# A fused attention and expert kernel: eleven and five relu buffers in the bias stage, conversions that begin later in two blocks, and gating rows one step later

## The chip, the core and the metric

The kernel runs on one core of a Trainium2 chip. The metric is the device time in microseconds (us) of one execution. The core has five engines that each work through their own instructions in program order: TensorE (PE in the profile; its weight loads are PEld), VectorE (DVE), ScalarE (ACT), GpSimd (POOL), and SyncE, whose queue (SPq) issues nearly all transfers of this kernel. Engines wait for each other through semaphores, so an instruction that waits holds up everything behind it on the same engine.

## The reference, cut to what matters

Three parts follow each other. Attention with a computed position bias:

```python
x = (psi_rel / psi_i)[..., None]            # (576, 576, 1)
bias = np.maximum(x @ w1 + b1, 0.0) @ w2    # hidden 32, 8 heads
scores = scale * q @ k.T + bias.transpose(2, 0, 1)[None]
attn = softmax(scores); attn_out = attn @ v # batch 4, heads 8, seq 576, dim 64
```

Then a mixture of 8 experts that picks the best expert of each token and weighs the result by two gates, and then a dense layer pair on 2304 tokens:

```python
e_idx = argmax(x @ w_gate); gate_w = softmax(x @ w_gate)[e_idx]
out[t] = gate_w[t] * sigmoid(x @ w_output_gate)[e] * (relu(x @ w1[e]) @ w2[e])
h = x @ w_in; out = (h * cos(h)) @ w_out     # 512 -> 2048 -> 512, weights in float64
```

## The kernel before

**Bias stage** (`bias_table`). For 36 groups of rows, in the order ROWS, it makes four relu tiles of up to 128 x 576 (L379 on ACT into buffers hhA, L381 on DVE into buffers hhD), multiplies them with w2 on PE (L391), copies the result to a buffer `ev` on ACT (L363, five buffers in turn) and sends it to the table Bd in DRAM (L364). There are 8 buffers hhD and 4 hhA. The pools p0 (W, cc, bp), p0h (hhD, hhA) and p0e (ev) lie one behind the other in SBUF. When the stage ends they are given up, and attention's pools p1s (s, e, et) and p1e (eT0, eT1) take the same addresses. A tile that takes over an address waits for the last user of that address, which for `ev` is the transfer L364. By tile sizes (per partition): W, cc, bp 3,744 bytes; one hh 2,304; one ev 2,368; p1s 25,312; one eT 12,800. So eT0 lies at 25,312 to 38,112 of this region and eT1 at 38,112 to 50,912, and the five ev at 31,392 to 43,232. The last row group (position 35) uses the first ev buffer.

**Attention** (`attention`). 16 pairs n (two heads hp of a batch b) of 5 units u each. One pass over a unit: scores on PE (L524), bias add and row minimum on DVE (L534), then for the unit before it transposes on PE (L560) and copies of them into eT0 or eT1 on ACT and DVE (L571, L573), exponentials on ACT (L545), the product with V on PE (L607), and the transposed rests (L593, L599). PSUM holds the scores of one unit, so the scores of the next unit wait for this unit's L534. Pair 0's bias comes from Bd by L440 and L443; its split into high and low parts runs on POOL.

**Later** is a list of work with due times. `later.step()` moves the clock by one and runs what is due: nine steps per pair (two in units 0 to 3, one in unit 4), then one for each step of the expert block. Work due at 0 and at 1 after it is queued runs in the same step. `Later` also holds chains, which `drip` emits a few instructions at a time and `drain` emits at once.

**Gating** (`Gating.queue`) is queued for batch b when the last product with V of its last pair is made, in unit 2 of the pair behind it (pairs 10, 12 and 14 for b = 0, 1, 2; for b = 3 just ahead of the expert block). Its parts: `sums` (DVE, L186 to L189: reciprocals rs of the row sums), `rows` (PE L196 and L197 turn rs, ACT L199 and L200 copy it to the buffer lp, SP sends it to Fd), `factors` (loads F from Fd, L207), `scale` (L213), `logits0` (PE L224, ACT L225 into lp), `logits1` (L232, L233) and the chain `choose`, which ends with L295 on PE and the copy L297 on ACT into lp. There is one buffer lp. `logits0` of batch b first drains the chain of b - 1.

**Conversions** (`Doubles.half`). The weights of the last part come as float64 in 64 pieces. A piece takes two halves: L712 and L714 on DVE; L717 and L719 on DVE, L721 on POOL, a store (L722) and the load of a later piece (L701) on SP. Attention takes 24 pieces: `convert` emits 4 halves in a pair (CV_AT). The expert block takes the other 40.

**Expert block** (`moe_dense`). 64 steps s of 12 matmuls of layer 1 (L854) and 12 of layer 2 (L873, two steps behind). ACT (L858) and DVE (L859) turn a step's output into high and low parts, and L803 splits weights on DVE. A counter `dense.cost` adds planned DVE time; from step CONVERT_AT on, halves of 0.73 are emitted as long as the counter stays within STEP:

```python
while cv and cv.u < cv.end and (dense.cost + 0.73 <= STEP or least > 0):
```

The last part (`moe2`, PE work by L1379 and L1419) is not touched.

Of the kernel before, what the change touches and what calls it, by code (L numbers as in the profile page):

```python
# [9 lines left out]
F32 = mybir.dt.float32  # L10
# [9 lines left out]
B, H, S, D = 4, 8, 576, 64  # L20
# [100 lines left out]


SPREAD_AT, PAUSE = 40, (10, 14)
GATE_AT = (4, 4, 11, 12, 10, 11, 17, 18, 20), (4, 4, 5, 6, 5, 6, 7, 8, 12)


class Gating:
# [42 lines left out]
    def queue(self, later, b):  # L170

        at = GATE_AT[b == B - 1]
        p = [(0, self.sums), (1, self.rows)]
        p += [(at[i], lambda b, i=i: self.factors(b, i)) for i in range(NP_)]
        p += [(at[4 + i], lambda b, i=i: self.scale(b, i)) for i in range(NP_)]
        p += [(at[8] + i, lambda b, i=i: (later.drain(b - 1), self.logits0(b, i))) for i in range(2)]
        p += [(at[8] + 2, self.logits1),
              (at[8] + 3, lambda b: later.chains.append((b, self.choose(b))))]
        start = max(0, self.clear - later.now)
        self.clear = later.now + start + 12  # L180
        later.add([(dt, lambda fn=fn: fn(b)) for dt, fn in p], start)
# [124 lines left out]
def reach(G):  # L306

    return 16 * G + 15, S - 16 * G
# [23 lines left out]
def bias_table(tc, h, Bd, first, after):  # L332


    nc = tc.nc
    NQ = S // 4
    with tc.tile_pool(name="p0", bufs=1) as c, \
         tc.tile_pool(name="p0h", bufs=10) as hp_, \
         tc.tile_pool(name="p0e", bufs=5) as ep, \
         tc.tile_pool(name="p0ps", bufs=3, space=PSUM) as pp:  # L340
        W = c.tile([128, S], F32, name="W")
        cc = c.tile([128, 34 + NQ + S // 16], F32, name="cc")
        near, far = slice(0, 336), slice(336, S)
        nc.sync.dma_start(out=W[:, near], in_=h["t_rel"][:, near])
        nc.scalar.dma_start(out=cc, in_=h["cc"])
        nc.sync.dma_start(out=W[:, far], in_=h["t_rel"][:, far])
        first()
        w1c, b1c, w2b, psi, rp8 = cc[:, 0:1], cc[:, 1:2], cc[:, 2:34], cc[:, 34:34 + NQ], cc[:, 34 + NQ:]
        bp = c.tile([128, NQ], F32, name="bp")
        nc.vector.tensor_scalar(out=bp, in0=psi, scalar1=b1c, scalar2=None, op0=ALU.mult)  # L350
        slope = lambda t: nc.vector.tensor_scalar(out=W[:, t], in0=W[:, t], scalar1=w1c, scalar2=None, op0=ALU.mult)
        slope(near)
        pss = {}

        def evac(G):
            back, ahead = reach(G)
            ev = ep.tile([128, S + 15], F32, name="ev")
            ps, zero = pss.pop(G)
            parts = [(ev[:, 0:back + ahead], ps[:, zero - back:zero + ahead])]
            if G in MIRROR:  # L360
                parts = [(ev[:, 0:back], ps[:, 1:back + 1][:, ::-1]), (ev[:, back:back + ahead], ps[:, 0:ahead])]
            for dst, src in parts:
                nc.scalar.activation(out=dst, in_=src, func=AF.Copy, scale=rp8[:, G:G + 1])  # L363
            nc.sync.dma_start(out=Bd[:, 16 * G:16 * G + 16, S - 1 - back:S - 1 + ahead].rearrange("h i j -> i h j"),  # L364
                              in_=ev[:, 0:back + ahead])
            after(G)

        for at, G in enumerate(ROWS):
            ps = pp.tile([128, 1024], F32, name="ps")
            back, ahead = reach(G)  # L370
            n = max(back + 1, ahead)
            hs = []
            for ct in range(4):
                m = 4 * G + ct
                e = BIAS_ON[m]
                hh = hp_.tile([128, S], F32, name="hh" + e, bufs=dict(D=8, A=4)[e])
                hs.append(hh)
                if e == "A":
                    nc.scalar.activation(out=hh[:, 0:n], in_=W[:, 0:n], func=AF.Relu, bias=bp[:, m:m + 1], scale=1.0)  # L379
                else:  # L380
                    nc.vector.tensor_scalar(out=hh[:, 0:n], in0=W[:, 0:n], scalar1=bp[:, m:m + 1], scalar2=0.0,  # L381
                                            op0=ALU.add, op1=ALU.max)
            zero = 512 if max(back, ahead) <= 512 else back
            cuts = sorted({zero - back, zero, 512, zero + ahead})
            if G in MIRROR:
                zero, cuts = 0, [0, n]
            pss[G] = ps, zero
            for c0, c1 in zip(cuts, cuts[1:]):
                for ct in range(4):
                    x = hs[ct][:, c0 - zero:c1 - zero] if c0 >= zero else hs[ct][:, zero - c1 + 1:zero - c0 + 1][:, ::-1]  # L390
                    nc.tensor.matmul(ps[32 * ct:32 * ct + 32, c0:c1], w2b, x, start=True, stop=True)  # L391
            if at == 2:
                slope(far)
            if at >= 2:
                evac(ROWS[at - 2])
        evac(ROWS[-2])
        evac(ROWS[-1])


def attention(tc, h, ident, dram, xT, bpool, ps_t, gate, later, dense, cv):  # L400
# [3 lines left out]
    with ExitStack() as ctx:  # L404
# [90 lines left out]
        def first():  # L495
            load(0)
            load_v(0)

        bias_table(tc, h, Bd, first, after)
        sp, ep = pool("p1s", 3, **rw), pool("p1e", 1, **rw)  # L500
        ps_s, ps_a = pool("ps_s", 2, space=PSUM, **rw), pool("ps_a", 1, space=PSUM)
        gate.pa = [ps_a.tile([128, 512], F32, name=f"pa{g}") for g in range(2)]
        ET = []
        for g in range(2):
            e = ep.tile([128, 5, 2, 320], F32, name=f"eT{g}")
# [109 lines left out]
                        later.add([(SPREAD_AT, lambda: (later.drain(b), gate.spread(b)))])  # L615

        def convert(n, u):
            for _ in range(CV_AT[u] if cv and n < 12 else 0):
                cv.half()

        seq = [(n, u) for n in range(len(pairs)) for u in range(NU)]
# [3 lines left out]
        while t <= len(seq) or av:  # L625
            n, u = seq[t] if t < len(seq) else (None, None)
# [43 lines left out]
            if n is not None:  # L670
                if u < 4:
                    convert(n, u)
                    later.step()
                later.drip(2)
# [6 lines left out]
CV_AT = (0, 1, 0, 1, 2)  # L681
# [281 lines left out]
            later.step()  # L963


STEP, CONVERT_AT = 3.1, 6
X_AT, X2_AT, ADD_AT, GROUP_AT, HALF_AT, NEXT_AT = 21, 34, 48, 57, 60, 61
W1_AT = (3, 17, 39, 49)
W2_AT = (7, 21, 44, 53)
# [548 lines left out]
```

## Time and profile before

| what | value |
|---|---|
| median of 3 runs | 984.64 us (983.89 to 988.12) |
| profiled execution: own time | 988.05 us |
| profiled execution: span from first to last instruction | 986.3 us |
| mean granted TensorE clock, share of 2.4 GHz | 0.976 |
| PE busy in the span | 939.6 us (95%) |
| DVE busy | 663.5 us (67%) |
| ACT busy | 547.1 us (55%) |

The span has four stages: bias 0 to 46 us, attention 46 to 326 us, the expert block 326 to 579 us, the last part 579 to 986 us. In a line of the timeline the numbers ahead are start and duration; what stands in brackets at the end is how long the engine had been idle before it and what ended that.

### The profile page before, as it was taken

To read this page: it belongs to the slowest core of one execution; us is meant where nothing else is said; L and a number is where in the kernel's file an instruction comes from. 1 tells how busy PE (TensorE), PEld (TensorE's weight loads), DVE (VectorE), ACT (ScalarE), POOL (GpSimd) and SP (SyncE) were. 2 spreads that over 40 slices of the span, in tenths; PEclk is the share of its full clock that TensorE was granted. 3 is DMA by queue.
4 is the path that set the end of the run, shared out by engine and by line. 5 is a ranking of instruction groups with operands and counts; after the bars stand their busy time and mean duration, and the time that the engine had idled before them with its cause. 6 is when DMAs were issued, how large, how long until landed. Compare 5 with 4: busy or idle time off the path is not lost.

```text
span 986.3 us, 19359 instructions
## 1 busy us (share of the span) xinstructions
PE 939.6 (95%) x7185; PEld 794.1 (81%) x7186; DVE 663.5 (67%) x1498; ACT 547.1 (55%) x1171; POOL 303.7 (31%) x414
## 2 busy tenths in 40 slices
PE   7979999989989896999999999999999999999997
PEld 4656666666666695999989998999999989999996
DVE  8958888988676466887658989654454454544542
ACT  8947777777667522335234377545455454554443
POOL 0034554545344211221321114324224233232222
PEclk9969999999999997999999999999999999999999
DMA  7965536643525393553765734010010010100001
GB/s 217 284 204 190 156 126 211 197 135 115 163 87 173 104 298 132 185 179 118 219 226 191 265 119 137 22 64 1 1 64 1 18 47 1 64 1 1 33 1 37
DMA packets 62101, 118.07 MB, mean 120 GB/s; under 512 B 6649, under 2 KB 21261, under 8 KB 61997
## 3 DMA queue, kind: packets, MB, share of 16 engines
q1 hardware_dynamic: 61708, 116.58, 36.8%
q8 instruction: 59, 0.97, 0.4%
q14 instruction: 46, 0.37, 0.1%
q10 hardware_dynamic: 288, 0.16, 0.1%
HBM read 83.11 MB, written 33.60 MB: 118 GB/s over the span
## 4 chain that ended last, share of the span: by engine, by line
PE 67%; DVE 5%; issue 2%; DMA 2%; ACT 1%; POOL 1%; SPq 0%; DVEq 0%; ACTq 0%; POOLq 0%
PE ph L1379 20%; PE py L1419 20%; PE pl L854 8%; PE po L873 8%; PE ps_s L524 2%; PE pa L607 2%; DMA F<-Fd 1%; PE Tp L560 1%; DVE s L534 1%; PE Tp L1151 1%; PE Tp L1160 1%; DMA raw<-in_w_in 1%; DVE xT L213 0%; DVE f32a L714 0%; DVE w0l L803 0%
## 5 line engine op out<-in xcount | busy, mean ns | idle before, releaser
L1405 POOL TENSOR_TENSOR gl<-tg,gh 128x384 fp32r<-128x384 f32 x96 | 97.8, 1019 | 280.6 <-ACT gh L1404 166.9
L1314 ACT ACTIVATE tk<-ph,magic 128x384 f32<-128x384 f32 x96 | 55.6, 579 | 159.0 <-PE ph L1379 158.5
L1319 DVE TENSOR_SCALAR tk<-tk 128x384 f32<-128x384 f32 x96 | 36.8, 383 | 154.2 <-ACT tk L1314 154.2
L1379 PE MATMUL ph<-xh,w0l 128*128 128x384 f32 x384 | 129.5, 337 | 0.0
L1379 PE MATMUL ph<-xh,w0h 128*128 128x384 f32 x384 | 129.2, 336 | 0.0
L1379 PE MATMUL ph<-xl,w0h 128*128 128x384 f32 x384 | 129.2, 336 | 0.0
L545 ACT ACTIVATE e<-s,mn 128x576 f32<-128x576 f32 x144 | 110.2, 768 | 9.1 <-DVE mn L534 8.6
L721 POOL TENSOR_TENSOR f32a<-f32a,raw 128x256 f32<-128x256 f32 x64 | 48.2, 754 | 212.7 <-DVE raw L719 171.3
L1419 PE MATMUL py<-w1h,gl 128*128 128x512 f32 x288 | 113.2, 393 | 0.0
L1419 PE MATMUL py<-w1h,gh 128*128 128x512 f32 x288 | 113.0, 392 | 0.0
L1419 PE MATMUL py<-w1l,gh 128*128 128x512 f32 x288 | 112.9, 392 | 0.0
L534 DVE CUSTOM_DVE_ANT_0 s<-ps_s,Bp 128x576 f32<-128x576 f32 x112 | 80.9, 755 | 35.2 <-PE ps_s L524 28.9
L607 PE MATMUL pa<-eT,V 128*64 128x256 f32 (+1 forms) x640 | 96.4, 423 | 0.0
L524 PE MATMUL ps_s<-HL 64*128 64x288 f32 x768 | 78.7, 324 | 6.6 <-DVE mn L534 4.3
L524 PEld LDWEIGHTS ps_s<-HL 64*128 64x128 f32 x768 | 59.6, 195 | 29.2 <-DVE mn L534 12.7
L854 PE MATMUL pl<-xh,w0h 128*128 128x288 f32 x256 | 79.9, 312 | 1.4 <-ACT xh L825 1.0
L858 ACT ACTIVATE hh<-pl 128x288 fp32r<-128x288 f32 x64 | 26.3, 411 | 99.0 <-PE pl L854 98.9
L854 PE MATMUL pl<-xl,w0h 128*128 128x288 f32 x256 | 76.3, 298 | 0.4 <-DVE xl L827 0.4
L854 PE MATMUL pl<-xh,w0l 128*128 128x288 f32 x256 | 76.1, 297 | 0.0
L873 PE MATMUL po<-hh,w1l 128*128 128x288 f32 x256 | 75.7, 296 | 0.0
L873 PE MATMUL po<-hh,w1h 128*128 128x288 f32 x256 | 75.7, 296 | 0.0
L873 PE MATMUL po<-hl,w1h 128*128 128x288 f32 x256 | 75.6, 295 | 0.0
(223 smaller groups left out, 2253.7 us busy)
## 6 DMA issues: line engine op xcount, KB each, us to landing
Bp<-in_w SPq DMA_DIRECT2D x38, 512.0 KB, 5.2
Bd<-ev SPq DMA_DIRECT2D x36, 295.5 KB, 3.6
Rqk<-in_qk SPq DMA_DIRECT2D x16, 576.0 KB, 6.4
raw<-in_w_in SPq DMA_DIRECT2D x32, 256.0 KB, 4.1
raw<-in_w_out SPq DMA_DIRECT2D x32, 256.0 KB, 3.2
Bp<-Bd SPq DMA_DIRECT2D x28, 288.0 KB, 6.8
X<-xT SPq DMA_DIRECT2D x7, 1152.0 KB, 5.3
V<-in_v SPq DMA_DIRECT2D x16, 320.0 KB, 4.5
```

What stands on the lines that cost most here:

```text
L524: nc.tensor.matmul(p[:, hf, :HF], w, y, start=(x == 0), stop=(x == 2))
L534: nc.vector.tensor_tensor_reduce(out=h2(s), in0=ps[:, :, :HF], in1=h2(bias(hp, i)), scale=-0.125, scalar=3e38, op0=ALU.add, op1=ALU.min, a ...
L545: nc.scalar.activation(out=e[:, par, :], in_=s, func=AF.Exp, bias=mn, scale=-1.0, accum_out=acc)
L607: nc.tensor.matmul(pa[64 * par:64 * par + 64, :W], d["V"][:, k, par, :], ET[g][:, k, par, :W], start=(k == 0), stop=(k == 4))
L721: self.tc.nc.gpsimd.tensor_tensor(out=af[:], in0=af[:], in1=low, op=ALU.add)
L854: nc.tensor.matmul(ps[:, :HF], w[:, c, :], x[:, c, :], start=(n == 0), stop=(n == 3 * NP_ - 1))
L873: nc.tensor.matmul(self.acc[d][:, :HF], w[:, ds_], x, start=(f == 0 and n == 0), stop=(f == self.FC - 1 and n == 2))
L1314: nc.scalar.activation(out=k, in_=hh, func=AF.Identity, scale=INV2PI, bias=magic)
L1319: nc.vector.tensor_scalar(out=k, in0=k, scalar1=-MAGIC, scalar2=None, op0=ALU.add)
L1379: nc.tensor.matmul(ps[:, :GT], w[:, c, :], x[:, c, :], start=(n == 0), stop=(n == 3 * NP_ - 1))
L1405: nc.gpsimd.tensor_tensor(out=lo, in0=g, in1=hi.bitcast(F32), op=ALU.subtract)
L1419: nc.tensor.matmul(acc[t], x[:, ts_], w, start=(f == 0 and n == 0), stop=(f == FC - 1 and n == 2))
```

## The change

Five edits: the relu buffers hhD go from 8 to 11 and hhA from 4 to 5, which moves the five `ev` buffers up by 9,216 bytes; the conversions of attention run in pairs 1 to 12 and not in 0 to 11; `rows` is due 2 steps after `sums` is queued and not 1; `logits0`, `logits1` and `choose` of batches 0 to 2 come one step later (20 to 21); conversions in the expert block begin at step 10 and not 6, with a planned fill of 3.2 and not 3.1 per step.

```diff
-GATE_AT = (4, 4, 11, 12, 10, 11, 17, 18, 20), (4, 4, 5, 6, 5, 6, 7, 8, 12)
+GATE_AT = (4, 4, 11, 12, 10, 11, 17, 18, 21), (4, 4, 5, 6, 5, 6, 7, 8, 12)
...
-        p = [(0, self.sums), (1, self.rows)]
+        p = [(0, self.sums), (2, self.rows)]
...
-                hh = hp_.tile([128, S], F32, name="hh" + e, bufs=dict(D=8, A=4)[e])
+                hh = hp_.tile([128, S], F32, name="hh" + e, bufs=dict(D=11, A=5)[e])
...
-            for _ in range(CV_AT[u] if cv and n < 12 else 0):
+            for _ in range(CV_AT[u] if cv and 0 < n < 13 else 0):
                 cv.half()
...
-STEP, CONVERT_AT = 3.1, 6
+STEP, CONVERT_AT = 3.2, 10
```

## Rows read from the trace of the kernel before

**Rows 1.** Windows: stretch: length, busy us (instructions) by engine, PE clock, DMA share, GB/s.

```profile
4.70:46.00 41.30, 41.02 (x556) 25.66 (x560) 41.30 (x117) 38.76 (x69) 0.00 (x0) 1.00 0.85 261
50.00:72.00 22.00, 15.24 (x132) 11.49 (x134) 12.15 (x29) 10.03 (x24) 7.25 (x13) 0.61 0.62 204
365.00:400.00 35.00, 26.66 (x186) 24.15 (x186) 24.04 (x70) 10.58 (x21) 6.44 (x7) 0.85 0.41 136
400.00:450.00 50.00, 49.48 (x376) 49.03 (x375) 43.40 (x120) 19.28 (x37) 14.99 (x15) 1.00 0.63 195
578.80:986.30 407.50, 400.91 (x2016) 363.53 (x2015) 216.97 (x403) 211.10 (x429) 119.76 (x116) 1.00 0.10 31
```

**Rows 2.** Waits of the whole span: engine, line, waited for: total us, times, longest.

```profile
PE pa L196 <- DVE rs L187: 6.0, 3, 2.1
```

**Rows 3.** Timeline of pair 0 of attention, 49 to 66 us.

```profile
49.86 0.76 SPq L364 DMA_DIRECT2D Bd<-ev  x1
...
50.67 2.57 SPq L440 DMA_DIRECT2D Bp<-Bd  x3
...
53.94 2.48 PE L524 MATMUL ps_s<-HL 64*128 64x288 f32 x12
...
56.73 0.60 ACT L571 ACTIVATE eT<-Tp 128x512 f32<-128x512 f32 x1 [4.21 <-DMA Bd<-ev]
...
62.48 0.29 DVE L712 TENSOR_SCALAR f32a<-raw 128x256 int32<-128x256 int32 x1 [4.94 <-DMA raw<-in_w_in]
62.80 0.42 DVE L714 SCALAR_TENSOR_TENSOR f32a<-raw,f32a 128x256 int32<-128x256 int32 x1
63.15 0.75 DVE L534 CUSTOM_DVE_ANT_0 s<-ps_s,Bp 128x576 f32<-128x576 f32 x1
```

**Rows 4.** Source L440 up to 62 us: time of the bias loads from issue to landing.

```profile
DMA to landing us min/median/max: 4.0/6.6/6.8
```

**Rows 5.** Timeline of DVE in pair 9: L534 of units 2 and 3.

```profile
201.11 0.76 DVE L534 CUSTOM_DVE_ANT_0 s<-ps_s,Bp 128x576 f32<-128x576 f32 x1 [0.66 <-PE ps_s L524]
...
204.19 0.76 DVE L534 CUSTOM_DVE_ANT_0 s<-ps_s,Bp 128x576 f32<-128x576 f32 x1 [0.23 <-ACT xT L610]
```

**Rows 6.** Timeline of pair 10, units 2 and 3.

```profile
216.40 0.76 DVE L534 CUSTOM_DVE_ANT_0 s<-ps_s,Bp 128x576 f32<-128x576 f32 x1 [0.67 <-PE ps_s L524]
...
220.47 0.71 PE L196 MATMUL pa<-ident,rs 128*8 128x128 f32 x5 [2.13 <-DVE rs L187]
...
222.98 0.76 DVE L534 CUSTOM_DVE_ANT_0 s<-ps_s,Bp 128x576 f32<-128x576 f32 x1 [2.43 <-PE ps_s L524]
```

**Rows 7.** Timeline of pair 14, units 3 and 4.

```profile
295.11 0.76 DVE L534 CUSTOM_DVE_ANT_0 s<-ps_s,Bp 128x576 f32<-128x576 f32 x1 [2.63 <-PE ps_s L524]
...
296.69 0.27 ACT L297 ACTIVATE lp<-pa 5x128 f32<-5x128 f32 x1 [2.37 <-DMA Fd<-lp]
...
301.57 0.76 DVE L534 CUSTOM_DVE_ANT_0 s<-ps_s,Bq 128x576 f32<-128x576 f32 x1 [4.41 <-PE ps_s L524]
```

**Rows 8.** Timeline of PE in the first steps of the expert block.

```profile
331.28 1.23 PE L196 MATMUL Tp<-ident,rs 128*8 128x128 f32 x5 [2.01 <-DVE rs L187]
...
333.08 0.61 PE L854 MATMUL pl<-xh,w0h 128*128 128x288 f32 x1
```

**Rows 9.** Timeline of the expert block, steps 6 to 11: DVE and PE.

```profile
357.47 0.76 DVE L213 TENSOR_TENSOR xT<-xT,F 128x576 f32<-128x576 f32 x1 [3.46 <-DMA F<-Fd]
...
363.30 0.88 DVE L714 SCALAR_TENSOR_TENSOR f32a<-raw,f32a 128x256 int32<-128x256 int32 x1
...
370.98 0.29 DVE L712 TENSOR_SCALAR f32a<-raw 128x256 int32<-128x256 int32 x1 [2.70 <-DMA raw<-in_w_in]
...
375.07 0.39 PE L269 MATMUL Tp<-oh,ones 128*128 128x40 f32 x2 [3.86 <-DVE oh L256]
...
378.16 0.19 DVE L272 TENSOR_REDUCE cnt<-Tp 128x8 f32<-128x40 f32 x1
...
379.94 0.37 PE L295 MATMUL Tp<-ident,cs 128*5 128x128 f32 x1 [4.48 <-DVE cs L289]
```

## The prediction

> **What bounds the kernel now.** I read the windows by stage first [rows 1]. In the last part PE is busy 400.91 of 407.5 us, with nothing of the change in it, and at 400 to 450 us, deep in the expert block, 49.48 of 50. In both PE sets the end, so an edit can gain there only what PE idles: almost nothing. In the bias stage DVE is busy all 41.30 us and PE follows it. What is left is three places where PE stands still: pair 0 of attention (50 to 72 us: 15.24 of 22, clock 0.61), the gating rows of each batch, and steps 9 to 12 of the expert block (365 to 400 us: 26.66 of 35, clock 0.85). The list of waits names the second kind: PE waits for rs, the row sums' reciprocals, 6.0 us in three places [rows 2]. Then I read the timelines of these places, in order of time.
>
> **Pair 0.** The exact chain [rows 3]: the last ev transfer is issued at 49.86; ACT's first copy into eT0 waits until 56.73 for it, since eT0 (25,312 to 38,112) lies on ev buffers, the first of which (31,392 to 33,760) is the one sent last. DVE's copy waits too. Behind that copy DVE has the first conversion half, which waits until 62.48 for raw, and behind this the L534 of unit 2, at 63.15, though PE had its scores ready at 56.4 (53.94 + 2.48).
>
> More relu buffers put ev at 40,608 to 52,448. eT0 then overlaps only relu buffers, whose readers are matmuls that are over; eT1 still overlaps ev, so POOL's clearing of eT1 still waits for the last transfer, with the copies of the rests queued behind it on POOL. Leaving conversions out of pair 0 takes the raw wait away. Next late is the bias itself: three loads share the issue from 50.67 to 53.24 and land 6.6 us after issue [rows 3, 4], so the second of them (51.5) at about 58.1. That is the new bound of unit 2, where 63.15 was: 63.15 - 58.1 = 5.0. Units 3 and 4 follow at the pace of matmuls at half clock; I keep **4.7** us. Of this the conversions alone would give about 3 (ACT's exponentials of unit 1 still stand behind the late copy at 56.73), the moved ev alone nothing, since DVE would still stand at 62.48. Bounds: 2, when the loads land at the worst of [rows 4] and PE's rests come as late as now, and 7.5, when the whole gap of 62.48 - 57.5 and half a unit more disappear. In the bias stage itself the buffers give 0: DVE makes the tiles without a gap [rows 1] and never waits for a free one. If DVE had such waits, three more buffers would save them.
>
> **Gating rows in attention.** A usual step from the L534 of unit 2 to that of unit 3 is 204.19 - 201.11 = 3.08 us [rows 5]; with the rows between them it is 222.98 - 216.40 = 6.58 [rows 6]. The reason stands in the order: sums and rows run in the same step, PE's L196 waits 2.13 for rs and the scores of unit 3 are queued behind it. One step later, L196 stands behind scores and transposes. PE then makes the scores while DVE makes rs, and unit 3's L534 comes when DVE has done rs, at 220.5: 222.98 - 220.5 = 2.4 gained. L196's own 0.71 us and ACT's two copies of lp are still paid, now ahead of the exponentials of unit 3; I keep **2.0** for pair 10. The pattern stands three times [rows 2]. In pair 12 the logits of batch 0 follow, and they too start behind fewer waits: **2.5**.
>
> Pair 14 has more: the chain of batch 0 ends there, and its L297 writes lp, which the transfer Fd still reads, so ACT stands 2.37 us and unit 4 comes 301.57 - 295.11 = 6.46 us behind unit 3 [rows 7]. The chain's last instruction keeps its place, right behind the L534 of unit 3, so now L297 comes first and the rows wait for the transfer of its lp (Cd, taken to be as long as Fd: 2.37). Two things cover this: the copy of transposes, and the transfer's own start before PE has turned rs. About 1 us of ACT stays open. The logits, again one step behind the rows, have unit 3's exponentials between them and the rows on ACT. I take 2.4 at unit 3 and 1.3 more at unit 4: **3.7**. For all three pairs 8.2; bounds 3 (all waits move behind lp but for 1 us each) and 14 (the 3.5 of [rows 6] three times, and 3.4 of the 6.46).
>
> **Conversions moved to pair 12.** Four halves, two DVE instructions each, 0.29 + 0.42 for the first kind [rows 3], so 4 x 0.71 = 2.8 us of DVE, with their loads and stores on SP. They fill DVE's time beside PE; one stands between units 1 and 2, one behind unit 3, two behind unit 4, and a softmax can slip behind one. I charge **0.7**, one half; bounds 0 and 2.8.
>
> **Start of the expert block.** Batch 3's L196 waits 2.01 for rs at 331.28, and layer 1 of step 1 begins only at 333.08 [rows 8]. Moved behind step 1's matmuls, the wait is covered by their work. The 0.71 to 1.23 us of L196 remain. **2.5**, that is the wait and part of the matmuls at half clock behind it; bounds 0 (the F loads behind it come later and nothing is won) and 3.8.
>
> **Steps 6 to 12 of the expert block.** Here DVE is behind: it waits 3.46 for F, runs ten halves from step 6 on, and waits 2.70 for a raw piece at 370.98. The chain of batch 2 is queued behind, and PE, which drains it ahead of batch 3's logits, waits 3.86 at L269 and 4.48 at L295 [rows 9]: 8.34 us, nearly all that PE idles at 365 to 400 [rows 1]. With CONVERT_AT 10 the raw pieces have long landed and steps 6 to 9 hold no halves (before: 2, 3, 3, 2 by the counter), so DVE catches up by step 9. Batch 2's chain comes one step later (21 for 20), and the drain stays at step 11: six of its parts are ahead of it and not twelve. Then L269 waits perhaps 0.4, but L295 waits for 17 small DVE instructions of about 0.19 [rows 9], 3.2 us, of which 0.5 run beside L269: 2.7. So 8.34 - 0.4 - 2.7 = 5.2. The clock: 0.85 over 35 us means 10.5 us at the lower level, 8.3 of it idle, so 2.2 us of work at half rate, 1.1 us lost, mostly given back; and PE's small waits for late low parts. Together **6.5**; bounds 0 and 9.5. The fill of 3.2 puts one more half into 15 steps between 12 and 47 (worked out with the counter's rule) and the last half falls in step 56, not 62. That costs 0 as long as DVE has room: 43.40 of 50 us are taken [rows 1], and PE needs a step's low part only two steps later. Without that cover each is 0.7 us.
>
> **A rule against the fill.** L714 takes 0.42 alone [rows 3] and 0.88 where POOL's L721 of the half before runs beside it [rows 9]. The Trainium skill, page "SBUF — State Buffer", section "Who interferes with whom", says a DVE instruction with two SBUF inputs contends with a GpSimd instruction that reads SBUF, and the later one blocks until the other is done. The trace agrees, by these two numbers. By the row alone, 15 more halves that each meet an L721 take 15 x 0.46 = 6.9 us more of DVE; if none of it were covered, the sum would be 14.3.
>
> **Sum.** 4.7 + 8.2 + 2.5 + 6.5 - 0.7 = 21.2 us. The profiled execution took 988.05, so 966.9 for it. That execution lies 3.4 above the median of the runs, 984.64; taken from the median it is **963.5**, which I predict.
>
> **Rivals.**
> 1. The wait in steps 9 to 12 stays, since F and not the conversions holds DVE (3.46 us at 357.47, [rows 9]). For it: F lands late behind weight loads that do not move. Against: PE waits for none of it until the halves come. It takes 6.5 from the sum: 970.
> 2. The gating waits only move: the rows' copies and the transfers of lp stand ahead of the exponentials now. For it: ACT's 2.37 in [rows 7]. Against: the scores are no longer behind rs. It takes 7 of 8.2: 970.5.
> 3. The fill meets POOL, as above, uncovered: 970.4.
> 4. More goes than I sum: the gating pairs fall to the usual pace (14 for 8.2) and pair 0 too (7.5 for 4.7): 955.
> 5. The change doesn't do what it says: eT0 still meets ev, and each stall is replaced by the next: 980 to 988.
> 6. Slower: DVE becomes the bound of the expert block. Its place is steps 10 to 63, its price the DVE time by which a step passes PE's. It decides from 21.2 / 54 = 0.39 us per step on. Against it: 6.6 us are free in 50 [rows 1], 0.4 per step, and the new halves replace old ones. At 0.6 per step: 963.5 + 32 = 996.
>
> **How the numbers follow.** Chances: the forecast (958 to 968) 0.50, rival 1 0.13, rival 2 0.12, rival 3 0.07, rival 4 0.10, rival 5 0.05, rival 6 0.03. The range 954 to 976 holds the forecast and rivals 1 to 4, with the unknown costs from 2.8 us of halves to the worst landing; rivals 5 and 6 and a pile-up of two of the first are out. Within 0.5% means 979.7 to 989.6, about what a measurement of this kernel can tell from no change. Faster than that 0.92, within 0.04, slower 0.04.
>
> **What would show it.** Right: ACT's first L571 no longer waits for ev, L534 of unit 2 near 58; no L712 in pair 0; steps from unit 2 to 3 of pairs 10, 12, 14 near 4; the waits for rs gone from PE; L269 with almost no wait and L295 with some 2.7; the last part as long as now. Wrong: a wait for the bias loads beyond 60 us, ACT waiting for Cd in pair 14 for more than 1 us, PE waiting for L859 in steps 12 to 47.

## The result and the profile after

The changed kernel takes **971.43 us** (median of 4 runs, 967.98 to 973.71) against 984.88 for the kernel before in the same session. The ratio is **0.9855**, with a 95% interval of 0.9818 to 0.9892. That is 13.4 us, and faster by my own bound of 0.5%. I had predicted 963.5 with a range of 954 to 976. The sign and the range held, but the gain is two thirds of the 21.2 us that I had summed. In the profiled executions the span fell from 986.3 to 971.9 us, 14.4 us.

First the windows of the kernel after, the same stretches as in [rows 1] and two short ones (columns as there).

```profile
4.70:46.00 41.30, 41.01 (x556) 23.79 (x560) 41.30 (x117) 38.76 (x69) 0.00 (x0) 1.00 0.85 261
50.00:72.00 22.00, 19.88 (x191) 15.25 (x192) 12.65 (x34) 14.11 (x34) 7.59 (x16) 0.69 0.81 266
358.00:362.00 4.00, 0.54 (x4) 0.38 (x3) 3.75 (x21) 0.00 (x0) 1.26 (x1) 0.91 0.46 172
362.00:368.00 6.00, 6.00 (x25) 4.14 (x25) 2.56 (x7) 2.46 (x5) 2.85 (x3) 0.50 0.44 123
365.00:400.00 35.00, 35.00 (x262) 34.69 (x262) 26.54 (x69) 14.93 (x28) 9.25 (x9) 0.96 0.48 154
400.00:450.00 50.00, 47.72 (x346) 46.66 (x345) 43.70 (x109) 19.08 (x36) 12.23 (x14) 0.97 0.51 153
564.40:971.90 407.50, 401.01 (x2017) 363.64 (x2015) 215.42 (x403) 211.30 (x429) 120.59 (x116) 1.00 0.09 31
```

The bias stage and the last part are unchanged. Pair 0 has 19.88 us of PE work in its 22, where there were 15.24. The hole of steps 9 to 12 is shorter and lies at 358 to 362 now, but the 6 us behind it run at the lower clock level (0.50). New is 400 to 450 us: 47.72 busy, where PE had 49.48.

The waits of the whole span say the same by line (columns as in [rows 2]).

```profile
PE pa L224 <- ACT lp L200: 3.8, 2, 3.4
...
PE Tp L1118 <- DVE xb L1112: 1.8, 1, 1.8
```

L196's waits for rs in attention, 6.0 us in [rows 2], are gone from the top; L224's wait for L200 has come, and L1118's has grown (0.5 before).

**Step times.** The table below is worked out from the timelines: a pair is the time from its first L534 to that of the next pair, a step of the expert block is read at its L858 on ACT. All executions named later are in it. The ratio is to runs of the kernel before in the same session.

```
kernel       pair 0  pair 10  pair 12  pair 13  pair 14  steps 0-4  steps 8-12  steps 28-32  median   ratio (95%)
before         22.8     18.9     21.3     15.9     22.9       14.4        27.2         15.3  984.88
after          17.8     16.5     17.5     16.7     22.8       11.3        22.0         18.9  971.43   0.9855 (0.9818-0.9892)
only_ev        25.6     19.6     19.8     15.9     21.8       14.4        25.5         15.3  985.69   0.9997 (0.9982-1.0013)
only_conv      19.2     18.2     20.2     15.9     21.7       14.4        25.5         15.3  979.94   0.9941 (0.9920-0.9961)
only_gate      22.8     16.5     17.5     16.9     21.9       11.3        30.9         14.5  983.79   0.9980 (0.9965-0.9994)
only_dense     22.8     19.1     21.4     15.9     21.7       14.4        20.2         18.9  983.38   0.9987 (0.9971-1.0003)
after_cr       17.2     16.5     17.5     16.7     17.6       11.3        21.2         17.3  966.79   0.9810 (0.9793-0.9826)
after_store2   17.9     16.5     17.5     16.7     18.6       11.2        20.8         18.9  967.79   0.9818 (0.9787-0.9849)
before_cr      24.5     18.2     19.8     15.9     21.3       12.8        25.1         15.3  982.92   0.9966 (0.9944-0.9987)
after_s31c6    18.4     16.5     17.6     16.7     21.7       11.2        30.5         14.5  978.98   0.9918 (0.9901-0.9935)
after_s315     18.1     16.5     17.6     16.7     22.8       11.3        22.3         18.3  973.75   0.9860 (0.9824-0.9895)
after_mid31    17.2     16.5     17.5     16.7     21.7       11.2        19.3         15.3  968.79   0.9819 (0.9787-0.9852)
best_l14       17.0     16.5     17.5     16.7     17.7       11.2        14.4         15.8  968.16   0.9815 (0.9798-0.9831)
cr_mid31       18.2     16.5     17.5     16.7     17.6       11.2        22.1         15.3  964.56   0.9771 (0.9740-0.9802)
```

One execution's step has a scatter that depends on the stage: where no edit touches it, pair 0 varies by 1 to 2 us, pair 14 by 1.2, steps 8 to 12 by 3, pairs 10 and 12 of kernels with the old gating by 1.4 and 1.6, steps 0 to 4 and 28 to 32 by 1.6 (and 15.3 or 14.5 for the latter with the old fill). The rest repeats to 0.2. But for pair 0, most of this scatter goes with TensorE's clock. The windows of the same stretches give its mean granted share in each execution:

```
stretch       kernels                       us at mean granted clock
pair 10       old gating                    18.2 at 1.00, 18.9 to 19.6 at 0.91
              new gating                    16.5 at 1.00
pair 12       old gating                    19.8 to 20.2 at 1.00, 21.3 and 21.4 at 0.92
              new gating                    17.5 at 1.00
pair 14       old gating, one buffer lp     21.7 and 21.8 at 1.00, 22.9 at 0.85
              new gating, one buffer lp     21.7 to 21.9 at 0.92, 22.8 at 0.85
steps 0-4     old gating                    12.8 at 1.00 (before_cr), 14.4 at 0.88
              new gating                    11.2 to 11.3 at 1.00
steps 8-12    old gating, conversions       25.1 to 25.5 at 0.86 to 0.87, 27.2 at 0.82
              both new (not best_l14)       19.3 at 1.00, 20.8 and 21.2 at 0.92, 22.0 to 22.3 at 0.86
steps 28-32   fill 3.2                      17.3 at 1.00 (after_cr), 18.9 at 0.91
```

So a gain from before to after is partly the wait itself and partly a clock that no longer falls behind it. With the clock at 1.00 on both sides, pair 10 gains 1.7 us, pair 12 2.3 to 2.7 and steps 0 to 4 1.6. The intervals of the ratios from 0.981 to 0.986 overlap, so what a single later edit is worth is read from its column and not from the total.

From before to after the columns give pair 0 5.0, pair 10 2.4, pair 12 3.7, pair 13 -0.8, pair 14 0.1, steps 0 to 4 3.1, steps 8 to 12 5.1 and steps 28 to 32 -3.6. Outside of the table, pair 15 up to step 0 of the expert block took 24.5 and not 23.7 us. Forecast were 21.2; the two largest holes are pair 14 (3.7 expected) and steps 28 to 32 (nothing expected).

### The profile page after: what moved, and what is told of

Same layout as the page of the kernel before. It is cut to its first block, busy times and chain, and to the rows that moved or that the text cites. A ratio compares the mean times of both kernels' runs of the same rounds, so it can differ in the third digit from the quotient of the medians.

```text
span 971.9 us, 19358 instructions
## 1 busy us (share of the span) xinstructions
PE 937.1 (96%) x7185; PEld 791.1 (81%) x7186; DVE 661.7 (68%) x1498; ACT 547.5 (56%) x1171; POOL 305.8 (31%) x414
## 4 chain that ended last, share of the span: by engine, by line
PE 70%; DVE 5%; ACT 2%; issue 2%; DMA 1%; POOL 0%; SPq 0%; DVEq 0%; ACTq 0%; POOLq 0%
PE ph L1379 21%; PE py L1419 20%; PE pl L854 9%; PE po L873 9%; PE pa L607 2%; PE ps_s L524 2%; PE Tp L560 1%; DVE s L534 1%; PE Tp L1151 1%; ACT e L545 1%; PE Tp L1160 1%; DMA Cd<-lp 0%; DMA F<-Fd 0%; DVE w0l L803 0%; PE Tp L224 0%
## 5 line engine op out<-in xcount | busy, mean ns | idle before, releaser
L534 DVE CUSTOM_DVE_ANT_0 s<-ps_s,Bp 128x576 f32<-128x576 f32 x112 | 81.0, 755 | 32.8 <-PE ps_s L524 22.8
L721 POOL TENSOR_TENSOR f32a<-f32a,raw 128x256 f32<-128x256 f32 x64 | 48.1, 752 | 146.8 <-DVE raw L719 118.9
L858 ACT ACTIVATE hh<-pl 128x288 fp32r<-128x288 f32 x64 | 26.3, 412 | 100.9 <-PE pl L854 100.7
L524 PE MATMUL ps_s<-HL 64*128 64x288 f32 x768 | 75.9, 318 | 3.0 <-ACT ev L363 1.4
L524 PEld LDWEIGHTS ps_s<-HL 64*128 64x128 f32 x768 | 57.5, 191 | 24.8 <-DVE mn L534 9.2
```

The costliest lines, as they stand in the source:

```text
L524: nc.tensor.matmul(p[:, hf, :HF], w, y, start=(x == 0), stop=(x == 2))
L534: nc.vector.tensor_tensor_reduce(out=h2(s), in0=ps[:, :, :HF], in1=h2(bias(hp, i)), scale=-0.125, scalar=3e38, op0=ALU.add, op1=ALU.min, a ...
L721: self.tc.nc.gpsimd.tensor_tensor(out=af[:], in0=af[:], in1=low, op=ALU.add)
```

## The experiments

### One edit at a time

**The buffers alone.**

```diff
-hh = hp_.tile([128, S], F32, name="hh" + e, bufs=dict(D=8, A=4)[e])
+hh = hp_.tile([128, S], F32, name="hh" + e, bufs=dict(D=11, A=5)[e])
```

> The kernel before with the larger relu buffers alone (hhD 11, hhA 5). My theory: DVE still waits for raw behind the conversion half of pair 0, so L534 of unit 2 stays near 63 and the time stays 0 to 1 us below before. Rival: the copies into eT0 alone held pair 0, then most of its 5.0 us come back here and the conversions part gives nothing.

Measured: 0.9997, no change. The timeline of its pair 0 shows why.

```profile
52.60 0.60 ACT L571 ACTIVATE eT<-Tp 128x512 f32<-128x512 f32 x1 [0.55 <-PE Tp L560]
...
64.05 0.29 DVE L712 TENSOR_SCALAR f32a<-raw 128x256 int32<-128x256 int32 x1 [9.99 <-DMA raw<-in_w_in]
...
64.72 0.75 DVE L534 CUSTOM_DVE_ANT_0 s<-ps_s,Bp 128x576 f32<-128x576 f32 x1
```

ACT's first copy comes at 52.60 without the wait for ev that stood in [rows 3]. DVE then stands behind L712 for 9.99 us, and unit 2 begins later than before. The freed time went into the next wait on the same engine.

**The conversions of attention alone.**

```diff
-            for _ in range(CV_AT[u] if cv and n < 12 else 0):
+            for _ in range(CV_AT[u] if cv and 0 < n < 13 else 0):
```

> The kernel before with the conversions in pairs 1 to 12 alone. My theory: ACT's first L571 still waits for ev until about 56.7, DVE no longer waits for raw; L534 of unit 2 between 58 and 60, 2 to 4 us gained in pair 0 and under 1 lost in pair 12. Rival: the two waits of pair 0 hide each other fully, then nothing is gained unless both go.

Measured: 0.9941, 5.8 us. Pair 0 took 19.2 us (3.6 gained), and DVE's timeline has the other wait still in it:

```profile
57.97 0.69 DVE L573 COPY eT<-Tp 128x512 f32<-128x512 f32 x1 [2.51 <-DMA Bd<-ev]
58.58 0.76 DVE L534 CUSTOM_DVE_ANT_0 s<-ps_s,Bp 128x576 f32<-128x576 f32 x1
```

So the two edits of pair 0 are worth nothing and 3.6 alone, and 5.0 together. Unit 2 begins 7.6 us behind the pair's first L534 here, and 7.3 in the changed kernel; what the moved ev adds lies behind it (unit 3 follows after 5.4 us here and after 3.8 there). The rest of the 5.8 us lies in columns that scatter (pairs 12 and 14, steps 8 to 12), and I don't count it as the edit's.

**The gating alone.**

```diff
-GATE_AT = (4, 4, 11, 12, 10, 11, 17, 18, 20), (4, 4, 5, 6, 5, 6, 7, 8, 12)
+GATE_AT = (4, 4, 11, 12, 10, 11, 17, 18, 21), (4, 4, 5, 6, 5, 6, 7, 8, 12)
...
-        p = [(0, self.sums), (1, self.rows)]
+        p = [(0, self.sums), (2, self.rows)]
```

> The kernel before with the gating rows one step later and the logits one step later, alone. From the trace of the changed kernel: pair 10 gains 2.3, pair 12 some 4, the start of the expert block 3.1, pair 14 about 0 and pair 15 loses 0.8; together 8 to 9 us by the start of the expert block. Its steps 9 to 12 still hold ten halves from step 6, so PE's waits at L269 and L295 stay near 8 us: total 8 to 9 us under before. Rival: the logits one step later (21 for 20) and not the conversions emptied L269; then 12 to 13 us.

Measured: 0.998, some 2 us, and not 8 to 9. In its trace 8.5 us are won between the first L534 of pair 10 and step 8 of the expert block (139.24 us against 147.77), but steps 8 to 12 take 30.9 us, 3.7 more than before. DVE and PE there:

```profile
365.08 0.30 DVE L712 TENSOR_SCALAR f32a<-raw 128x256 int32<-128x256 int32 x1 [2.38 <-DMA raw<-in_w_in]
...
369.65 0.29 DVE L712 TENSOR_SCALAR f32a<-raw 128x256 int32<-128x256 int32 x1 [3.03 <-DMA raw<-in_w_in]
...
371.83 0.19 DVE L242 TENSOR_REDUCE mx<-L 128x5 f32<-128x40 f32 x1
...
375.46 0.62 PE L269 MATMUL Tp<-oh,ones 128*128 128x40 f32 x2 [9.21 <-DVE oh L256]
```

DVE waits 2.38 and 3.03 us for raw pieces, all of batch 2's chain (from L242 on) is queued behind these halves, and PE waits 9.21 us at L269 (3.86 in [rows 9]). The first of the two waits stood before the change too (2.70). The second is new, and the edit brings it about: with the chain a step later the counter puts three halves into step 9 and not two, and the third needs a piece that the kernel before took up in step 10, at 376.36, without a wait. That is eleven halves in steps 6 to 9, and not the ten that I expected. The rest of the difference to 8.5 us lies in four places: the bias stage (pair 0 begins 1.7 later in this execution), pair 3 (1.4, told at the end), steps 16 to 28 (1.1) and the last part (0.7); 0.8 comes back at steps 28 to 32.

**The expert block's conversions alone.**

```diff
-STEP, CONVERT_AT = 3.1, 6
+STEP, CONVERT_AT = 3.2, 10
```

> The kernel before with conversions from step 10 and the fill of 3.2 alone. My theory: PE's waits at 365 to 400 fall by 4 to 5 us, and the fuller steps cost 3 to 4 us again in the second half of the expert block, where Extra.gather (L1111, L1112, L1118) stands behind DVE: total 0 to 2 us under before. Rival: the late loss has another cause (batch 3's gating one step later), then 4 to 6 us under before.

Measured: 0.9987, which is not told apart from no change. Inside, steps 8 to 12 gain 7.0 us and steps 28 to 32 lose 3.6, the same 3.6 as in the changed kernel: the late loss belongs to this edit and not to the gating.

The four parts alone sum to 0.95% (0.03, 0.59, 0.20 and 0.13), together they give 1.45%. The profile shows where they need each other: in pair 0, and in steps 8 to 12, where gating and conversions give -3.7 and +7.0 alone and +5.1 together.

**All edits but the last.**

```diff
-STEP, CONVERT_AT = 3.2, 10
+STEP, CONVERT_AT = 3.1, 6
```

> The changed kernel with STEP, CONVERT_AT = 3.1, 6 again, so all edits but the last. With the gating alone PE's wait at L269 grew from 3.86 to 9.21, since halves at steps 7 to 11 held DVE on raw pieces; theory: the same here, steps 8 to 12 take 30 to 31 us instead of 22, the loss at steps 28 to 32 is gone, total 4 to 6 us above the changed kernel. Rival: parts just add; then the last edit is worth what it was alone, 1 to 2 us.

Measured: 978.98 us, 0.9918, that is 0.63% or 6 us behind the changed kernel. Steps 8 to 12 took 30.5 us and steps 28 to 32 14.5, as expected. The edit that is worth 1.3 us alone is worth 6 beside the others.

### Pair 14

In the changed kernel the pair's timeline runs like this.

```profile
281.20 0.59 SPq L215 DMA_DIRECT2D X<-xT  x1
281.46 0.27 ACT L297 ACTIVATE lp<-pa 5x128 f32<-5x128 f32 x1 [0.36 <-PE pa L295]
281.83 0.69 SPq L298 DMA_DIRECT2D Cd<-lp  x1
282.03 0.71 PE L196 MATMUL pa<-ident,rs 128*8 128x128 f32 x5
...
282.14 0.76 DVE L534 CUSTOM_DVE_ANT_0 s<-ps_s,Bp 128x576 f32<-128x576 f32 x1
...
286.19 0.59 ACT L199 ACTIVATE lp<-pa 8x512 f32<-8x512 f32 x1 [3.49 <-DMA Cd<-lp]
...
287.05 1.94 PE L224 MATMUL pa<-xT,g 128*32 128x512 f32 x8 [3.40 <-ACT lp L200]
...
290.87 0.76 DVE L534 CUSTOM_DVE_ANT_0 s<-ps_s,Bq 128x576 f32<-128x576 f32 x1 [6.69 <-PE ps_s L524]
```

The wait for rs is gone: L196 runs at 282.03 with nothing in front. But ACT's copy of the rows stands 3.49 us until Cd has left the buffer lp, L224 waits for that copy, the scores of unit 4 are queued behind L224, and unit 4 comes 290.87 - 282.14 = 8.73 us behind unit 3 (6.46 in [rows 7]). Cd was issued at 281.83, 4.36 us before its release, right behind the 1.15 MB store of X. This is the sign of being wrong that the prediction names, ACT waiting for Cd for more than 1 us.

**A buffer of its own for the small tile.**

```diff
-cr = self.c.tile([128, S], F32, name="lp")[0:5, 0:128]
+cr = self.t([128, S], "F")[0:5, 0:128]
```

> The changed kernel with the small tile of L297 (5x128, sent to Cd) in a buffer of F instead of the one buffer lp. Theory: pair 14 gains nothing from the later rows since ACT's L199 waits 3.49 us for Cd behind a large store; without that wait, unit 4 follows unit 3 after 4 to 5 us instead of 8.73, and the total falls by 3.5 to 5 us. Rival: the matmuls of the rows and logits themselves and the lower clock make those 8.73 us; then the step stays above 7 and the total within 1.5 us.

Measured: 966.79 us, ratio 0.9810; pair 14 took 17.6 us, 5.2 less, and ACT no longer waits for a transfer:

```profile
281.15 0.76 DVE L534 CUSTOM_DVE_ANT_0 s<-ps_s,Bp 128x576 f32<-128x576 f32 x1
...
282.16 0.59 ACT L199 ACTIVATE lp<-pa 8x512 f32<-8x512 f32 x1 [0.44 <-PE pa L196]
...
285.22 0.76 DVE L534 CUSTOM_DVE_ANT_0 s<-ps_s,Bq 128x576 f32<-128x576 f32 x1 [2.02 <-PE ps_s L524]
```

Unit 4 follows unit 3 after 4.07 us. The matmuls of rows and logits are all still there, so they are not what made 8.73. The windows of the whole pair, in the changed kernel and here, show what the 5.2 us are (columns as in [rows 1]):

```profile
272.29:295.11 22.82, 19.42 (x208) 12.38 (x206) 12.32 (x40) 13.67 (x34) 8.17 (x15) 0.85 0.37 119
271.30:288.94 17.64, 16.90 (x208) 11.11 (x206) 12.31 (x40) 13.51 (x34) 7.95 (x14) 1.00 0.31 107
```

PE idles 2.7 us less, and the same 208 matmuls take 2.5 us less, since the clock does not fall any more (0.85 and 1.00). So the rival's lower clock was there, but as a consequence of the wait.

**The store two steps later.** With the one buffer lp kept, only the order of two transfers on SP's queue changes in pair 14.

```diff
+        p += [(at[7] + 2, self.store)]
...
-        if hp == NP_ - 1:
-            nc.sync.dma_start(out=self.X1[b], in_=self.xT[:, :, b, :])
+    def store(self, b):
+        self.tc.nc.sync.dma_start(out=self.X1[b], in_=self.xT[:, :, b, :])
```

> The changed kernel with the store of a batch's X (L215, 1.15 MB) two steps later, so that in pair 14 the small transfer Cd is issued just ahead of the store and not just behind it. Theory: Cd takes 4.4 us from issue to release there because it shares the queue with the store; ahead of it some 2.3 to 2.7 us as Fd in the kernel before, so ACT's L199 waits about 1.5 us for it instead of 3.49, unit 4 comes some 2 us earlier and the total is 1.5 to 2.5 us lower. Rival: the 4.4 us are the cost of this transfer wherever it stands; then L199 waits 3.5 us again. The F loads and the expert block's first weight loads may meet the store instead, for up to 2 us.

Measured: 967.79 us, ratio 0.9818; pair 14 took 18.6 us, 4.2 less, twice what I expected.

```profile
281.50 0.29 SPq L298 DMA_DIRECT2D Cd<-lp  x1
...
281.89 0.60 SPq L215 DMA_DIRECT2D X<-xT  x1
...
283.16 0.59 ACT L199 ACTIVATE lp<-pa 8x512 f32<-8x512 f32 x1 [0.72 <-DMA Cd<-lp]
...
286.23 0.76 DVE L534 CUSTOM_DVE_ANT_0 s<-ps_s,Bq 128x576 f32<-128x576 f32 x1 [2.30 <-PE ps_s L524]
```

Ahead of the store the same transfer is done after 1.66 us and not 4.36, and ACT waits 0.72. So Cd was late for its place behind the store. The Trainium skill, page "DMA: Bandwidth & Descriptors", section "Queues, rings and completion order", says that each DMA engine works through the descriptors of a ring in order. The trace agrees, by 1.66 and 4.36. The expectation was too small for two reasons: Cd by itself is faster than the Fd from which I had taken 2.3, and I had left out the clock. PE is busy 16.90 us at a clock of 1.00 in this pair, 2.5 less than in the changed kernel; only 1.7 of the 4.2 are idle time.

**The kernel before with the small tile apart** (the same diff on the kernel before).

> The kernel before with the tile of L297 in F alone. If the later rows gain in pair 14 what I forecast once the buffer is apart (3.7 us), the pair takes about 21 us here, against 17.6 with both. If the wait for the one buffer was all of the pair's loss before too, it takes 18 to 18.5 here. The total 1 to 4 us under before.

Measured: 982.92 us, ratio 0.9966; pair 14 took 21.3 us. With the buffer apart, the later rows take the pair from 21.3 to 17.6: 3.7 us, the size that I had forecast for the change as it was. A part of it is again the clock (0.92 over the pair here, 1.00 with both), for which the forecast had no term in this pair.

### Steps 28 to 32

The changed kernel there (the columns of a timeline; POOL, DVE, ACT and PE in order of time):

```profile
425.52 1.67 DVE L803 TENSOR_TENSOR w0l<-Bp,w0h 128x1024 fp32r<-128x1024 f32 x1
426.07 2.41 POOL L813 TENSOR_TENSOR xT<-xT,Cb 128x576 f32<-128x576 f32 x1
427.12 1.51 DVE L712 TENSOR_SCALAR f32a<-raw 128x256 int32<-128x256 int32 x1
...
428.51 0.69 ACT L825 ACTIVATE xh<-xT 128x576 fp32r<-128x576 f32 x1 [4.01 <-POOL xT L813]
429.11 0.58 ACT L1111 ACTIVATE xb<-Tp 128x512 fp32r<-128x512 f32 x1
...
429.74 0.50 PE L1118 MATMUL Tp<-xb,xc 128*128 128x512 f32 x1 [0.50 <-ACT xb L1111]
431.29 0.68 DVE L1112 TENSOR_TENSOR xb<-Tp,xb 128x512 fp32r<-128x512 f32 x1
...
432.02 0.51 PE L1118 MATMUL Tp<-xb,xc 128*128 128x512 f32 x1 [1.78 <-DVE xb L1112]
```

`gather` needs L1111 and L1112 within a step, and PE has L1118 queued ahead of the next layer 1. DVE comes to L1112 only at 431.29, PE waits 0.50 and 1.78 us, and the clock falls behind it (0.97 over 400 to 450). In after_cr, with the same code there, PE waits the same 0.49 and 1.79 us and the clock stays. The windows of steps 28 to 32, after and after_cr:

```profile
420.90:439.76 18.86, 16.58 (x110) 15.86 (x109) 18.52 (x33) 7.79 (x13) 5.94 (x6) 0.91 0.40 119
413.14:430.44 17.30, 15.02 (x110) 14.31 (x109) 16.99 (x31) 7.78 (x12) 5.94 (x6) 1.00 0.40 120
```

So of the 3.6 us that the changed kernel loses here 1.6 are the clock and 2.0 the late DVE. DVE is busy 18.52 of 18.86. Which halves are to blame?

**The fill at 3.15.**

```diff
-STEP, CONVERT_AT = 3.2, 10
+STEP, CONVERT_AT = 3.15, 10
```

> The changed kernel with the fill at 3.15 and not 3.2; by the counter's rule that takes one half each out of steps 29 and 30 of the expert block (and out of 13 and 45, 46), and the last half falls in step 62 again. Theory: the 3.6 us that the changed kernel loses between steps 28 and 32 come from these halves (they make DVE's L1112 and ACT's L1111 late for PE's L1118, and the clock falls behind the stall); without them 3 to 4 us gained. Rival: POOL's L813 beside DVE is the cause and not the number of halves; then under 1 us.

Measured: 973.75 us, ratio 0.9860, no gain; steps 28 to 32 took 18.3 us. The theory fell as I had put it: the halves of steps 29 and 30 are not the cause. That did not yet make POOL the cause, since at 3.15 steps 26 and 28 still hold one half more than before. The trace of this run speaks against L813 and the L712 beside it:

```profile
424.85 1.61 POOL L813 TENSOR_TENSOR xT<-xT,Cb 128x576 f32<-128x576 f32 x1
...
431.05 0.50 PE L1118 MATMUL Tp<-xb,xc 128*128 128x512 f32 x1 [1.79 <-DVE xb L1112]
```

L813 takes 1.61 us and not 2.41, no L712 near it takes more than 0.29, and PE waits 1.79 us for L1112 all the same. What meets POOL here is the L714 of the half that step 28 holds more: it takes 0.93 us, against 0.42 alone, beside an L721.

**The fill at 3.1 in steps 24 to 31 alone.**

```diff
-            while cv and cv.u < cv.end and (dense.cost + 0.73 <= STEP or least > 0):
+            while cv and cv.u < cv.end and (dense.cost + 0.73 <= STEP - 0.1 * (24 <= s < 32) or least > 0):
```

> The changed kernel with the fill 0.1 lower (3.1) in steps 24 to 31 of the expert block alone; by the counter's rule steps 26, 28, 29 and 30 then hold one half less each, as before the change, and two more fall in step 62 or near. With 3.15, which left out 29 and 30 alone, steps 28 to 32 took 18.3 us against 18.9 (15.3 before). Theory: the halves of 26 and 28 put DVE a step behind before L1112; now these steps take 14.5 to 15.5 us, and the total falls by 3 to 4. Rival: POOL's L813 beside DVE is enough by itself; then above 17 and under 1.5 us gained.

Measured: steps 28 to 32 took 15.3 us, as before the change, and L1118 waits as long as before:

```profile
PE Tp L1118 <- DVE xb L1112: 0.5, 1, 0.5
```

The ratio is 0.9819. Of the 7 us between the profiled spans (964.8 and 971.9) 3.6 are this stretch; steps 8 to 12 and pair 14, in the columns that scatter, hold most of the rest. By the counter step 31 has a half less too, but that one would come behind the wait. What differs from the fill of 3.15 ahead of L1112 are the halves of steps 26 and 28, so these put DVE behind; which of the two counts for more was not tried. L813 beside DVE is not what decides between these two runs: it takes 1.60 us here and 1.61 at the fill of 3.15, and the L803 beside it 2.07 in both. Nor is it enough by itself: in after_s31c6, L813 took 2.40 us and L712 beside it 1.51, as in the changed kernel, and L1118 waited for nothing (steps 24 to 28 had taken 1.2 us more there). Whether the halves alone, without any POOL beside DVE, would do it was not tried.

### Two mends together, and one that only moved a wait

> Both mends together: the tile of L297 in F, and the fill 3.1 in steps 24 to 31. If they add: pair 14 near 17.6 us, steps 28 to 32 near 15, some 963 us, 7 to 8 under the changed kernel. If the later one is lost behind something else: 966 to 967, as with the tile alone.

Measured: 964.56 us, ratio **0.9771** (0.9740 to 0.9802), against 0.9855 for the changed kernel: 0.84%, some 8 us. Pair 14 took 17.6 and steps 28 to 32 15.3 us, so the two mends add. This is the fastest of the kernels, some 22 us under the kernel before, about what I had forecast for the change itself.

The last wait of [rows 9], at L295, was tried together with the tile in F and the fill of 3.15:

```diff
-GATE_AT = (4, 4, 11, 12, 10, 11, 17, 18, 21), (4, 4, 5, 6, 5, 6, 7, 8, 12)
+GATE_AT = (4, 4, 11, 12, 10, 11, 17, 18, 21), (4, 4, 5, 6, 5, 6, 7, 8, 14)
```

> The changed kernel with the tile of L297 in F, the fill 3.15, and batch 3's logits and chain at 14 and not 12, so that batch 2's chain has two steps more before it is drained. Theory: besides 4 us at pair 14 and 3.5 at steps 28 to 32, PE's wait at L295 (3.3 us) and the stretch at half clock behind it go, 4 to 6 us more: 958 to 961 in all. Rival: the chain of batch 3 then ends later and its drain or the extra parts from step 21 on take the wait over; then 963 to 965.

Measured: 968.16 us, ratio 0.9815, no better than with the tile alone. Steps 8 to 12 went to 14.4 us, but steps 12 to 16 to 20.8, and PE still waits at L295:

```profile
363.61 0.27 PE L295 MATMUL Tp<-ident,cs 128*5 128x128 f32 x1 [3.35 <-DVE cs L289]
```

L269 ran there at 359.95 without a wait, but the rest of batch 2's chain began on DVE only at 361.84, behind splits and low parts, so PE stood for as long as before, two steps later. Steps 24 to 28 lost 3.4 us besides, and with steps 28 to 32 they took 32.3 us, about as long as in the changed kernel (32.0) and at the fill of 3.15 (31.4), against 28.4 before. So the loss that was to go is still there, but four steps earlier; what of it is batch 3's later chain was not tried apart.

## Why the prediction was right or wrong

**Pair 0: right.** Forecast 4.7, measured 5.0. Neither edit does it alone, as the exact chain said: nothing from ev, 3.6 from the conversions (forecast about 3). What comes next is the bias load, as forecast. The lines are of the changed kernel, but for the last, which is the same L534 in after_cr:

```profile
54.03 0.60 ACT L571 ACTIVATE eT<-Tp 128x512 f32<-128x512 f32 x1 [1.58 <-PE Tp L560]
...
57.28 0.76 DVE L534 CUSTOM_DVE_ANT_0 s<-ps_s,Bp 128x576 f32<-128x576 f32 x1 [2.19 <-PE Tp L560]
...
56.93 0.76 DVE L534 CUSTOM_DVE_ANT_0 s<-ps_s,Bp 128x576 f32<-128x576 f32 x1 [2.76 <-DMA Bp<-Bd]
```

In the changed kernel the view names PE's L560, whose end came last. But L534 does not read what L560 makes, and the first load of Bp, issued at 50.17, landed 7.0 us later, at 57.12. In all eight executions with both edits unit 2's L534 begins 0.16 us after this landing. I had put the bound at 58.1, from the second of the three loads; unit 2 needs the first.

**Pairs 10 and 12: right.** Forecast 2.0 and 2.5, measured 2.4 and 3.7, of which 1.7 and 2.3 to 2.7 remain when the clock is 1.00 on both sides; the rest is the fall of the clock behind the old wait, for which I had no term. From unit 2 to unit 3 it takes 4.2 and 3.9 us now (near 4 was forecast). L196 still waits, but behind the scores of unit 3, and ACT reaches the rows after that unit's L534 has begun:

```profile
215.32 0.70 PE L196 MATMUL pa<-ident,rs 128*8 128x128 f32 x5 [0.41 <-DVE rs L187]
215.43 0.76 DVE L534 CUSTOM_DVE_ANT_0 s<-ps_s,Bp 128x576 f32<-128x576 f32 x1
...
216.43 0.59 ACT L199 ACTIVATE lp<-pa 8x512 f32<-8x512 f32 x1 [0.92 <-PE pa L196]
```

The four halves moved into pair 12 cost nothing that shows: 17.5 us with them and 17.5 in only_gate without them; I had charged 0.7. What I did not charge is that logits moved by a step leave their pair: pair 13 took 0.8 us more, and the way from pair 15 to the expert block another 0.8, both in only_gate too (1.0 and 1.0).

**Pair 14: the step that failed.** I took 3.7, on Cd "taken to be as long as Fd: 2.37", with about 1 us of ACT left open. Measured 0.1. At unit 3 the gain came (6.44 us from unit 2 to 3 before, 3.86 after; I had taken 2.4), but unit 4, where I had taken 1.3 more, comes 2.3 later behind unit 3 than before. I had seen that the rows would wait for Cd, and looked at its length and not at its place: the last `scale` sends 1.15 MB on the same queue one instruction earlier, and Cd took 4.36 us. Two experiments show it from two sides (the buffer apart, the store behind), and before_cr gives 3.7 for the rest of the step, part of it clock. Rival 2, the gating's waits only move, held in this one of three pairs.

**Start of the expert block: right.** Forecast 2.5, the wait and part of the matmuls at half clock; measured 3.1 in steps 0 to 4, 1.6 at equal clock. L196 waits 0.43 where it waited 2.01 [rows 8], and the clock is 1.00 there and not 0.88.

**Steps 6 to 12: the mechanism right, the size short.** Forecast 6.5, measured 5.1, between executions that scatter (25.1 to 27.2 us with the old code, 19.3 to 22.3 with the new). L269 waits 0.20 us, as said (0.4):

```profile
358.25 0.39 PE L269 MATMUL Tp<-oh,ones 128*128 128x40 f32 x2 [0.20 <-DVE oh L256]
361.90 0.37 PE L295 MATMUL Tp<-ident,cs 128*5 128x128 f32 x1 [3.26 <-DVE cs L289]
```

L295 waits 3.26 and not 2.7, one of the small DVE instructions taking 1.05 us (L259). The larger miss is the clock: I had written 1.1 us of half-rate work, mostly given back. Behind a hole of 3.3 us it fell again: 362 to 368 us ran at 0.50, and work of 3 us took 6. Rival 1 is out: two waits for F are still there on DVE and PE waits for none of them.

**The fill: the other step that failed.** "That costs 0 as long as DVE has room", with the room read from 50 us of the trace (43.40 of 50). It cost 3.6 us. The room was a mean, and the halves of steps 26 and 28 fell where DVE has none: right behind them `gather` puts two L1112 beside the splits. I had named the price if the cover is gone, 0.7 a half, but a late DVE instruction in front of PE cost 2.0 us of delay and, in four of five executions, the clock behind it. Rival 3 put 6.9 us on it through POOL. POOL's part of the mechanism is seen in its rows: L712 takes 1.51 us beside L813, which takes 2.41, against 0.29 alone. The Trainium skill, page "SBUF — State Buffer", section "Who interferes with whom", says that DVE and GpSimd share one pair of ports, and that of two instructions that need it the one that issues first holds it for its whole instruction while the other blocks. The trace agrees, by these rows. But the wait comes with the halves where no L712 is drawn out (fill 3.15), and goes without them where L813 is the same (fill 3.1 in steps 24 to 31), so by the runs the halves decide. A part of their price is still POOL's: of the 1.2 us that the half of step 28 takes at the fill of 3.15, 0.5 are its L714 beside L721.

**The sum.** 21.2 forecast, 14.3 measured at the last steps of the expert block. Pair 14 lacks 3.6, the fill 3.6, steps 6 to 12 1.4 and the moved logits 1.6; pairs 0, 10, 12 and the start of the expert block gave 3.2 more than forecast, the 0.7 included; 2.2 of it lie in pairs 10 and 12 and at the start, where the clock gave more than that. The range held, but 971.43 lies outside 958 to 968, to which I had given one half. It lies near the times of rivals 1 to 3 (970 to 970.5), and that speaks for none of them: the first is out, the second held in one pair of three, and of the third POOL draws the halves out, but what they cost is the wait behind them. That the gating and the conversions of the expert block need each other, the prediction did not say: it priced them as if they simply added.

**What stays open:** why the clock falls in one execution and not in another behind the same waits (steps 28 to 32 of after and after_cr). The scatter of steps 8 to 12 (19.3 to 22.3 us over kernels with the same edits there) goes with it and with L295's wait: 2.38 us in the three shorter ones, 3.23 to 3.55 in the three longer. What makes that wait longer was not tried.

## What to carry to other kernels

When a wait is moved so that a small transfer decides, look at what is issued just ahead of it on its queue: the same Cd took 1.66 us ahead of a large store and 4.36 behind it. Room on an engine is read in the steps where work is added and not as a mean over fifty microseconds; one late instruction in front of PE costs its delay and often the clock behind it, so compare a stage's times together with its granted clock. When a view names an engine for a wait, check that the instruction reads what that engine made: the wait for the bias load stood under PE's name. And an edit tried alone can look worthless when it uncovers the next wait: the gating alone gave 2 us, while the last edit gave 1.3 alone (not told apart from nothing) and 6 beside the others.

## What the runs showed of the hardware

A DVE instruction beside POOL can take five times its usual time: L712 1.51 us for 0.29. The same happened by chance in pair 3, which took 16.4 to 16.7 us in four of these executions and 15.3 in all others: DVE waited there for a raw piece, and then L712, or in best_l14 the L714 behind it (1.52 for 0.42), met POOL's L469. In cr_mid31 that ran from 104.18 to 105.60:

```profile
104.24 1.50 DVE L712 TENSOR_SCALAR f32a<-raw 128x256 int32<-128x256 int32 x1 [0.90 <-DMA raw<-in_w_in]
```

The stall of 3.3 us at L295 was followed by 6 us of granted clock 0.50 in the changed kernel. In best_l14 a stall of 3.35 us, two steps later, was followed by less of it: 0.50 from 365 to 367 us and 1.00 from 368 on (mean clock 0.92 over the 20.7 us from 355.5 to 376.2). A stall of 2.38 us there was followed by a fall in after_cr and after_store2 (0.92 over steps 8 to 12) and by none in after_mid31 (1.00). So at equal code and nearly equal waits the price of a stall of PE differed from one execution to the next.
